# Weight blocks read in halves through attention's buffers, their size check read again beside the experts

## The chip, the cores and the metric

The kernel runs on one core of one Trainium2 chip. The metric is the device time of one execution in microseconds (us). The engines are TensorE (PE; its weight loads are PEld), VectorE (DVE), ScalarE (ACT), GpSimd (POOL) and SyncE (SP), which issues most DMAs. GpSimd has a DMA queue of its own.

## The reference

Three layers follow each other.

1. A recurrent attention for 4 batches, 8 heads, 768 steps and head size 48. A complex decay `a` is cut to a magnitude of at most 0.999; the state is `S = a * S + k v^T`, and the output is `y = q S` (its real part).
2. An MLP on the 3072 tokens of 384 numbers: `h = x @ w_in` (384 x 2048), `g = elu(h)`, `x = g @ w_out` (2048 x 384). Its two weights come as 64-bit floats.
3. A mixture of 8 experts: gates from `x @ w_gate` and a noise term, the two best experts of each token, and for each expert `relu(x @ w1[e]) @ w2[e]` (384 x 1024 and 1024 x 384), weighted and summed.

## The kernel before, in words

**Units.** Attention and MLP are cut into 12 units (6 chunks of 128 steps x 2 pairs of batches; `i` is the batch in a pair). For each unit there are pieces of work: `p` prepares the decay (a 3-buffer ring of tiles with the tag `pp`), `o` and `m` make phases and magnitudes, `a` makes the scaled keys and queries (KK, X), `b` makes scores (`sc`, tile P), the state's update (`kt`, `upd`, `upd2`; tiles KT, sx, s1), the outputs `y` and their transposed split into a high and a low part (`xt`, tiles xh and xl, from line 789). `f` is the MLP of the unit (`f_pieces`, line 817): for each of 8 steps `l1` (line 822) makes 256 rows of h and its elu in high and low parts (gh by ScalarE, gl by GpSimd, line 841), and `l2` (line 845), two steps behind, adds to the two output sums. `r` (line 954) routes the tokens of a chunk: it writes (token, gate) rows into a table in DRAM by indirect DMA (line 948).

**MLP weights.** There are 32 blocks of 128 x 384 numbers, 16 of w_in and 16 of w_out. `fetch` (line 475) issues one load of 384 KB on GpSimd's queue (line 487) into a `raw` tile. VectorE reduces the high words to their least magnitude (line 488, for the check that no weight is too small for the decoding) and decodes 64-bit floats to 32 bits in three steps (lines 471 to 473). `load_w_in` and `load_w_out` (lines 507 and 517) then split a block into a high and a low part: ScalarE copies the high part; TensorE forms `identity x raw - high` in PSUM (lines 513, 514, 525, 531), and ScalarE copies the low part out (lines 515, 532). For w_out the gate columns `w_out @ [w_gate, w_noise]` are added (three transposes, line 521, and three products, line 527). The raw tiles have the tags xh and xl, the decoded ones gh and gl, woT has the tag ge: these are buffers of the MLP. `EARLY` is 8, so that all blocks take this path and the class `x` is empty.

**Order.** `place` (line 1099) gives every piece a planned time in units from PAR, `settle` (line 1112) pushes pieces behind others by rules, and the pieces are emitted in that order. It fixes in which order tiles of one tag take its buffers. `arrange` (line 28) then orders the instructions of every engine and of SP: it simulates them with costs, takes among the ready ones that with the longest chain behind it (after the tile `gok` those of the experts' stage in order of emission), and ties each engine to that order. For a DMA it adds bytes / 190 to a common clock (line 334).

**Experts.** `e_weights` (line 1012) loads and splits an expert's weights an expert ahead; `e_slots` reads the table (line 1024), `e_rows` gathers rows (line 1035) and transposes them, `e_first` (line 1045) and `e_second` (line 1067) multiply, and rows are added to the output by indirect DMA. `check` (line 1257) stands before this stage: it reduces `guard` and `wbad`, sums over partitions by a small product and writes `flags`, which are read at the very end.

`zeros` (line 1150) fills the output and the last rows of xs by 28 DMAs from one tile with the tag yo.

The functions that the change touches, and what calls them:

Of the kernel before, what the change touches and what calls it, by code (L numbers as in the profile page):

```python
# [21 lines left out]
PAR = {'EARLY': 8, 'x': (-0.25, 0.3), 'w': (0.15, 1.0), 'p': (-0.25, 0.6), 't': (-0.2, 0.0), 'o': (-0.1, 0.2), 'm': (0.35, 0.15), 's': (0.1, 0.0), 'k': (1.0, 0.0), 'v': (0.1, 0.0), 'a': (1.2, 0.55), 'b': (1.45, 0.35), 'f': (2.1, 0.95), 'r': (2.5, 1.05), ('pr', 'p'): 1.0, ('o', 1): 0.3, ('b', 2): -0.3, ('m', 's', 7): -0.1, ('t', 2): -0.3, ('b', 's', 8): 0.1, ('p', 's', 4): 0.2, ('a', 11): -0.15, ('b', 11): -0.3, ('b', 's', 11): 0.4, ('o', 11): -0.15, ('b', 's', 6): -0.1, ('a', 1): -0.15, ('p', 1): -0.3, ('p', 's', 3): 0.1, 'z': (0.9, 0.0), 'q': (0.3, 0.0), ('b', 's', 1): 0.1, ('p', 0): 0.3, ('o', 2): -0.3, ('a', 's', 0): -0.3, ('a', 's', 4): -0.5, ('a', 's', 6): 0.1, ('a', 's', 2): 0.1, ('k', 0): 0.15, ('o', 's', 0): -0.2, ('a', 0): -0.3, ('b', 's', 4): -0.2, ('b', 's', 0): 0.2, ('b', 's', 7): -0.3, ('m', 11): -0.3, ('b', 's', 2): 0.0, ('pr', 't'): -0.5, ('f', 2): 0.15, ('b', 's', 10): 0.3, 'ring': '0000001111', 'bufs': (2, 2), ('t', 0): -0.45, ('a', 's', 3): 0.1, ('p', 's', 0): -0.1, ('f', 0): -0.15, ('pr', 'q'): 0.5, ('b', 's', 12): -0.2, ('t', 1): 0.3, ('b', 's', 5): 0.3, ('m', 's', 0): 0.2, ('pr', 'f'): -0.5, ('pr', 'x'): -1, 'fs': 0, ('q', 0): 0.45, ('a', 's', 1): 0.1, ('k', 1): 0.15, ('o', 0): -0.3, ('m', 's', 8): -0.2, ('q', 2): -0.3, ('v', 0): 0.15, ('p', 2): 0.15}  # L22
# [5 lines left out]
def arrange(tc):  # L28
# [268 lines left out]
    while done < len(heads):  # L297
# [60 lines left out]
def tile_kernel(ctx, tc, q, k, v, a_re, a_im, w_in, w_out, w_gate, w_noise, noise, w1, w2, qp, kp, vp, ap,  # L358
# [42 lines left out]
    minus = consts.tile([128, 128], F32R, name="minus")  # L401
    ts(minus, jp, 0.0, -1.0, op0=OP.is_equal, op1=OP.mult)
# [59 lines left out]
    wbad = consts.tile([128, 2, 2 * FB], F32, name="wbad")  # L462
# [823 lines left out]
    for e in range(E):  # L1286
# [3 lines left out]
        if e == 0:  # L1290
            e_slots(0, 1)
# [268 lines left out]
```

## Time and profile before

| what | us |
|---|---|
| runs | 1238.35, 1238.43, 1240.42; median 1238.43 |
| profiled execution, its own time | 1239.85 |
| its span, first to last instruction | 1238.1 |
| TensorE busy in it | 1164.2 |
| VectorE busy | 678.6 |
| ScalarE busy | 643.4 |
| GpSimd busy | 370.3 |

The span is 1.75 us shorter than the execution's own time, which includes what lies around it. Busy times are unions of an engine's records; records of TensorE and VectorE overlap at their ends. Sums of durations over a line count such overlaps twice.

### The profile page before, as it was taken

The numbers are of one execution on the slowest core, as the hardware profiler recorded it, in microseconds if no ns is written. First come the engines' busy times: TensorE is split into PE (matmuls) and PEld (weight loads), VectorE is DVE, ScalarE is ACT, GpSimd is POOL, SyncE is SP. The second block draws the span as 40 slices with busy tenths as digits, with TensorE's granted clock in tenths as the row PEclk, the third lists the DMA queues.
The fourth block names the chain that finished last, engine by engine and source line by source line (L and its number), as shares of the span: only waits on it lengthen the run. The fifth ranks groups of instructions, "written<-read, shape, count | busy, mean of one in ns | idle before, by whom it ended". The sixth has DMA issues, their size and how long they took to land.

```text
span 1238.1 us, 23439 instructions
## 1 busy us (share of the span) xinstructions
PE 1164.2 (94%) x9205; PEld 1076.3 (87%) x9205; DVE 678.6 (55%) x1454; ACT 643.4 (52%) x1299; POOL 370.3 (30%) x360
## 2 busy tenths in 40 slices
PE   4688999999999999999999999899999999999997
PEld 3466888989998999899899998889898989899996
DVE  5889887586575848658513364443434344343221
ACT  6887977767776766675544462332323233232211
POOL 2111111223215222412533633342424242424222
PEclk9788999999999999999999999899999999999999
DMA  5456423022020211201010142342424242433111
GB/s 200 148 171 199 151 80 94 16 89 68 29 74 23 80 53 59 73 23 46 15 40 14 52 135 81 117 132 87 135 89 139 84 136 83 139 99 90 37 45 34
DMA packets 64312, 107.10 MB, mean 87 GB/s; under 512 B 19967, under 2 KB 46310, under 8 KB 64192
## 3 DMA queue, kind: packets, MB, share of 16 engines
q1 hardware_dynamic: 50096, 65.65, 17.2%
q0 software_dynamic: 14096, 39.86, 10.6%
q8 instruction: 74, 1.21, 0.4%
q14 instruction: 46, 0.38, 0.1%
HBM read 86.98 MB, written 20.70 MB: 87 GB/s over the span
## 4 chain that ended last, share of the span: by engine, by line
PE 68%; issue 11%; DVE 9%; ACT 5%; POOL 4%; DMA 2%; POOLq 0%; SPq 0%; DVEq 0%; ACTq 0%
PE mpo L1077 18%; PE mph L1055 17%; PE y L855 12%; PE ph L831 11%; PE sc L759 2%; PE py L776 2%; POOL table L948 2%; PE mtp L1040 1%; POOL gl L841 1%; PE py L782 1%; PE pu L719 1%; POOL raw L487 1%; PE tp L606 1%; DMA xr<-xs,slots 1%; ACT ge L835 1%
## 5 line engine op out<-in xcount | busy, mean ns | idle before, releaser
L841 POOL TENSOR_TENSOR gl<-ge,gh 128x512 fp32r<-128x512 f32 x96 | 129.6, 1353 | 428.6 <-ACT gh L840 331.6
L1057 ACT ACTIVATE egh<-mph 128x320 fp32r<-128x320 f32 (+1 forms) x128 | 66.2, 517 | 233.2 <-PE mpo L1077 134.2
L1077 PE MATMUL mpo<-weh,egh 128*128 128x384 f32 (+1 forms) x448 | 152.4, 340 | 0.0
L1077 PE MATMUL mpo<-weh,egl 128*128 128x384 f32 (+1 forms) x448 | 152.1, 340 | 0.0
L1077 PE MATMUL mpo<-wel,egh 128*128 128x384 f32 (+1 forms) x448 | 151.8, 339 | 0.0
L855 PE MATMUL y<-woh,gh 128*128 128x400 f32 x384 | 138.8, 361 | 0.0
L855 PE MATMUL y<-woh,gl 128*128 128x400 f32 x384 | 133.0, 346 | 1.0 <-POOL gl L841 0.9
L855 PE MATMUL y<-wol,gh 128*128 128x400 f32 x384 | 131.6, 343 | 0.0
L837 DVE SCALAR_TENSOR_TENSOR ge<-ge,ph 128x512 f32<-128x512 f32 x96 | 65.4, 684 | 115.9 <-ACT ge L836 107.5
L1085 POOL DMA_INDIRECT out_dram<-ac,slots x56 | 55.7, 994 | 230.3 <-DVE ac L1082 206.6
L1058 DVE SCALAR_TENSOR_TENSOR egl<-mph,egh 128x320 fp32r<-128x320 f32 (+1 forms) x128 | 75.1, 586 | 86.3 <-ACT egh L1057 51.7
L1082 DVE SCALAR_TENSOR_TENSOR ac<-mpo,slots,ac 128x384 f32<-128x384 f32 (+1 forms) x49 | 30.2, 616 | 163.1 <-PE mpo L1077 163.1
L1008 ACT ACTIVATE weh<-raw 128x384 fp32r<-128x384 f32 x128 | 65.3, 523 | 87.5 <-PE mpo L1077 60.0
L831 PE MATMUL ph<-xh,wih 128*128 128x256 f32 x576 | 103.2, 288 | 3.0 <-DVE ge L837 3.0
L831 PE MATMUL ph<-xh,wil 128*128 128x256 f32 x576 | 100.1, 283 | 0.0
L831 PE MATMUL ph<-xl,wih 128*128 128x256 f32 x576 | 100.0, 282 | 0.0
L831 PEld LDWEIGHTS ph<-xh,wih 128*128 128x128 f32 x576 | 86.4, 189 | 6.0 <-DVE ge L837 4.3
L1009 DVE TENSOR_TENSOR wel<-raw,weh 128x384 fp32r<-128x384 f32 x128 | 73.0, 586 | 30.4 <-ACT weh L1008 23.5
L840 ACT ACTIVATE gh<-ge 128x512 fp32r<-128x512 f32 x96 | 60.0, 628 | 54.2 <-PE y L855 49.9
L835 ACT ACTIVATE ge<-ph 128x512 f32<-128x512 f32 x96 | 56.5, 593 | 60.0 <-PE ph L831 36.6
L1077 PEld LDWEIGHTS mpo<-wel,egh 128*128 128x128 f32 (+1 forms) x448 | 81.3, 182 | 2.9
L1077 PEld LDWEIGHTS mpo<-weh,egl 128*128 128x128 f32 (+1 forms) x448 | 81.2, 181 | 2.7
(199 smaller groups left out, 2703.2 us busy)
## 6 DMA issues: line engine op xcount, KB each, us to landing
raw<-in_moe_w_dram SPq DMA_DIRECT2D x128, 192.0 KB
nat_a<-in_a_rows_dram SPq DMA_DIRECT2D x24, 512.0 KB
raw<-in_moe_w_in_dram POOLq DMA_DIRECT2D x16, 384.0 KB
raw<-in_moe_w_out_dram POOLq DMA_DIRECT2D x16, 384.0 KB
q<-in_q_pairs_dram SPq DMA_DIRECT2D x24, 256.0 KB
k<-in_k_pairs_dram SPq DMA_DIRECT2D x24, 256.0 KB
vt<-in_v_rows_dram SPq DMA_DIRECT2D x24, 192.0 KB
out_dram<-zero SPq DMA_DIRECT2D x24, 192.0 KB
```

Source lines behind the costliest of these rows:

```text
L831: mm(ph[:, j, :], w[:, z, :], x[:, z, :], start=n == 0, stop=n == 3 * KD - 1)
L835: act(e, ph, AF.Relu, scale=-1.0)
L837: stt(e, e, -1.0, ph, op0=OP.add, op1=OP.max)
L840: act(gh, e, AF.Copy)
L841: nc.gpsimd.tensor_tensor(gl, e, gh.bitcast(F32), op=OP.subtract)
L855: mm(d["y"][i], g[:, j, i * L:(i + 1) * L], w, start=s == 0 and j == 0 and n == 0, stop=s == NS - 1 and j == 1 and n == 2)
L1008: act(w[0], raw, AF.Copy)
L1009: tt(w[1], raw, w[0].bitcast(F32), op=OP.subtract)
L1055: mm(ph[:, :n], w[:, z, :], x[:, z, :], start=k == 0, stop=k == 3 * KD - 1)
L1057: act(gs[0][:, f, :n], ph[:, :n], AF.Relu)
L1058: stt(gs[1][:, f, :n], ph[:, :n], 0.0, gs[0][:, f, :n].bitcast(F32), op0=OP.max, op1=OP.subtract)
L1077: mm(po[:m], x[:, f, o:o + m], w, start=k == 0, stop=k == 3 * FE - 1)
```

## The change

1. `fetch` loads a block in two halves of 192 columns on SP's queue. The raw halves take the attention's tags s15 (two of three; 4 buffers) and KT (one of three; 2 buffers), the decoded block takes pp (3 buffers), woT takes P. The reduction is gone from it, and so is `late`.
2. The low part is a subtraction on GpSimd (for the 16 gate columns on VectorE); the identity and minus products and the copies of the low part are gone.
3. The blocks are placed over 2.7 units instead of 1.0, and tied by rules only to the l1 and l2 steps that need them. The rule that put them ahead of the first `xt` is gone.
4. `upd2` is emitted right after `upd`. `zeros` takes the tag route and stands between the first and the second routing.
5. The planner's DMA rate is 300 instead of 190.
6. In the stage of experts 0 to 5, 6, 6, 6, 6, 6 and 2 blocks are loaded whole once more on SP's queue into six buffers, and VectorE reduces each to its least magnitude; the end of the check stands in expert 7.

```diff
-PAR = {'EARLY': 8, 'x': (-0.25, 0.3), 'w': (0.15, 1.0), ...
+PAR = {'w': (0.15, 2.7), ...
...
-    for new, old in (("mw", "wa"), ("mps", "psa"), ("mpo", "psf")):
+    for new, old in (("mw", "wa"), ("mps", "psa"), ("mpo", "psf"), ("mc", "wf")):
...
-                dma = max(dma, st + 600) + nbytes[z] / 190
+                dma = max(dma, st + 600) + nbytes[z] / 300
...
-    def fetch(piece, f, n, late):
-
-        tagf = "ge" if late else ("gh", "gl")[n % 2]
-        t = wf.tile([128, Dm], F32, name="wf", tag=tagf, bufs=2)
+    def fetch(piece, f, n):
+
+        t = wa.tile([128, Dm], F32, name="wf", tag="pp", bufs=3)
...
-        for z, (a, b) in enumerate(((0, 256), (256, Dm)) if late else ((0, Dm),)):
...
-                raw = wf.tile([128, Dm, 2], I32, name="raw", tag=("xh", "xl")[n % 2], bufs=2)
-            nc.gpsimd.dma_start(*piece(f, a, b, raw))
-            nc.vector.tensor_reduce(wbad[:, z, n:n + 1], raw[:, :, 1].bitcast(F32), axis=AX.X, op=OP.min,
-                                    apply_absolute_value=True)
-            decode(raw, t[:, a:b])
+        for z in range(2):
+            tag = ("s15", "s15", "KT")[(2 * n + z) % 3]
+            raw = wa.tile([128, Dm // 2, 2], I32, name="raw", tag=tag, bufs=2 if tag == "KT" else 4)
+            o = z * (Dm // 2)
+            nc.sync.dma_start(*piece(f, o, o + Dm // 2, raw))
+            decode(raw, t[:, o:o + Dm // 2])
         return t
...
+    def load_w_in(f):
         WI[f] = [wts.tile([128, KD, 128], F32R, name=f"wi{x}", tag="wi") for x in "hl"]
         hi, lo = (w.rearrange("p c f -> p (c f)") for w in WI[f])
+        raw = fetch(w_in_piece, f, f)
         act(hi, raw, AF.Copy)
-        p = psf.tile([128, Dm], F32, name="wlo", tag="ph" if late else "y2", bufs=2)
-        mm(p, ident, raw, start=True, stop=False)
-        mm(p, minus, hi, start=False, stop=True)
-        act(lo, p, AF.Copy)
+        nc.gpsimd.tensor_tensor(lo, raw, hi.bitcast(F32), op=OP.subtract)
...
+        act(wT.rearrange("p c f -> p (c f)"), p[:, :Dm], AF.Copy)
         for c in range(KD):
-            mm(p[:, Dm:], wT[:, c, :], wg[:, c, :], start=False, stop=False, skip_group_check=True)
+            mm(p[:, Dm:], wT[:, c, :], wg[:, c, :], start=c == 0, stop=c == KD - 1, skip_group_check=True)
         act(hi[:, :Dm], raw, AF.Copy)
+        nc.gpsimd.tensor_tensor(lo[:, :Dm], raw, hi[:, :Dm].bitcast(F32), op=OP.subtract)
         act(hi[:, Dm:], p[:, Dm:], AF.Copy)
-        mm(p, minus, hi, start=False, stop=True, skip_group_check=True)
-        act(lo, p, AF.Copy)
+        tt(lo[:, Dm:], p[:, Dm:], hi[:, Dm:].bitcast(F32), op=OP.subtract)
...
-        zero = wf.tile([128, Dm], F32, name="zero", tag="yo", bufs=1)
+        zero = wf.tile([128, Dm], F32, name="zero", tag="route", bufs=1)
...
-    rules += [(("w", 0), at("b", 0, "xt")), (at("a", 0, "qq", 1), ("x", 0)), (("x", 0), ("k", 1)), (("x", 0), ("q", 1)),
-              (("z", 0), at("f", 0, "fin"))]
-    for sx in range(EARLY, NS):
+    rules += [(("r", 0), ("z", 0)), (("z", 0), ("r", 1))]
+    for sx in range(NS):
...
+    def weights_seen(e):
+
+        if not wide or e > E - 3:
+            return
+        n = -(-2 * FB // (E - 2))
+        for f in range(e * n, min((e + 1) * n, 2 * FB)):
+            raw = M["c"].tile([128, Dm, 2], I32, name="seen", tag="seen", bufs=6)
+            nc.sync.dma_start(*(w_in_piece(f, 0, Dm, raw) if f < FB else w_out_piece(f - FB, 0, Dm, raw)))
+            SEEN.append((f, raw))
+
+    def weights_least():
+        while SEEN:
+            f, raw = SEEN.pop(0)
+            nc.vector.tensor_reduce(M["bad"][:, f:f + 1], raw[:, :, 1].bitcast(F32), axis=AX.X, op=OP.min,
+                                    apply_absolute_value=True)
...
     for e in range(E):
         if e + 1 < E:
             e_weights(e + 1)
+        weights_seen(e)
         e_first(e, 0)
+        weights_least()
+        if e == E - 1:
+            check_end()
```

## Rows read from the trace of the kernel before

**Rows 1.** The page, part 1: busy time, share of the span, instructions.

```profile
PE 1164.2 (94%) x9205; PEld 1076.3 (87%) x9205; DVE 678.6 (55%) x1454; ACT 643.4 (52%) x1299; POOL 370.3 (30%) x360
```

**Rows 2.** Stretches: length; PE, PEld, DVE, ACT, POOL busy; PE clock, DMA share, GB/s.

```profile
0.00:75.00 75.00, 46.02 (x267) 34.18 (x269) 54.70 (x130) 56.48 (x117) 14.39 (x32) 0.86 0.55 175
75.00:123.00 48.00, 39.31 (x286) 29.75 (x283) 46.52 (x106) 38.60 (x90) 6.99 (x13) 0.86 0.59 183
...
740.00:800.00 60.00, 54.08 (x295) 48.81 (x294) 27.69 (x90) 20.45 (x49) 21.99 (x22) 0.94 0.37 106
800.00:1238.10 438.10, 428.90 (x2385) 393.31 (x2383) 159.70 (x298) 114.86 (x245) 144.62 (x143) 0.99 0.32 95
```

**Rows 3.** Timeline of VectorE, 60 to 130 us: start, length, instruction.

```profile
76.92 1.28 DVE L763 TENSOR_TENSOR P<-sc,causal 128x512 f32<-128x512 f32 x2
...
105.57 0.36 DVE L471 TENSOR_SCALAR wf<-raw 128x384 uint32<-128x384 uint32 x1
105.84 0.55 DVE L488 TENSOR_REDUCE wbad<-raw 128x1 f32<-128x384 f32 x1
106.30 0.55 DVE L472 SCALAR_TENSOR_TENSOR wf<-raw,wf 128x384 uint32<-128x384 uint32 x1
...
127.86 0.34 DVE L741 TENSOR_TENSOR St<-sx,s 128x192 f32<-128x192 f32 x1
```

**Rows 4.** Lines 798 and 831: least, median, most ns; first and last start, us.

```profile
L798 DVE TENSOR_TENSOR xl<-tp,xh x24: 543/557/558, 112.6 to 659.2; 128x384 fp32r<-128x384 f32 x24
...
L831 PE MATMUL ph<-xh,wih x576: 274/282/388, 126.9 to 732.1; 128*128 128x256 f32 x192
```

**Rows 5.** Groups by line and form, 0 to 300 us: busy us, mean ns, idle before.

```profile
L488 DVE TENSOR_REDUCE wbad<-raw 128x1 f32<-128x384 f32 x32 | 17.4, 544 | 0.0
...
L513 PE MATMUL wlo<-wf,ident 128*128 128x384 f32 x32 | 17.2, 625 | 21.4 <-DVE wf L473 20.2 <-ACT wol L532 0.8 <-ACT wil L515 0.2
L525 PE MATMUL wlo<-wf,ident 128*128 128x384 f32 x32 | 16.6, 607 | 0.0
...
L514 PE MATMUL wlo<-wih,minus 128*128 128x384 f32 x16 | 11.2, 698 | 2.7 <-ACT wih L511 2.7
...
L531 PE MATMUL wlo<-woh,minus 128*128 128x400 f32 x16 | 7.2, 447 | 0.3 <-ACT woh L530 0.3
```

**Rows 6.** The chain that ended last, in order of time: start, length, work.

```profile
713.72 2.14 PE ph L831 x18
...
724.51 2.17 PE y L855 x12
```

**Rows 7.** Stretches of line 513 alone: PE and PEld busy, then as in rows 2.

```profile
75.00:123.00 48.00, 7.59 (x16) 2.65 (x16) 0.86 0.59 183
```

**Rows 8.** Groups by line and form, 123 to 200 us; last, a timeline row.

```profile
L673 DVE TENSOR_TENSOR KK<-KK,X 128x1024 f32<-128x1024 f32 x5 | 7.2, 1436 | 5.9 <-ACT X L582 5.9
...
L681 DVE TENSOR_TENSOR X<-X,E 128x1024 f32<-128x1024 f32 x4 | 5.9, 1487 | 0.0
...
L740 DVE TENSOR_TENSOR sx<-sx,al 128x384 f32<-128x384 f32 x5 | 3.8, 768 | 0.0
...
L565 DVE TENSOR_TENSOR nat_a<-nat_a,pc 128x384 f32<-128x384 f32 x4 | 3.3, 824 | 0.5 <-ACT pc L563 0.5
L739 DVE TENSOR_TENSOR s<-sx,al 128x384 f32<-128x384 f32 x5 | 2.8, 552 | 0.0
...
L841 POOL TENSOR_TENSOR gl<-ge,gh 128x512 fp32r<-128x512 f32 x9 | 13.1, 1455 | 76.2 <-ACT gh L840 76.2
...
159.55 2.29 DVE L673 TENSOR_TENSOR KK<-KK,X 128x1024 f32<-128x1024 f32 x1
```

**Rows 9.** Waits: who for whom; total us, times, longest us.

```profile
POOL raw L487 <- DVE wf L471: 46.0, 15, 7.2
```

**Rows 10.** The tile zero: its 24 DMAs to the output, ns, first and last start.

```profile
L1154 SPq DMA_DIRECT2D out_dram<-zero x24: 421/440/932, 73.9 to 143.2; - x24
```

**Rows 11.** The chain that ended last, in expert 0: start, length, work.

```profile
767.38 0.21 DMA slots<-table
```

More of the change, by code (lines that the diff above doesn't have):

```diff
@@ L461, in tile_kernel @@
     wide = w_in.dtype != F32
-    wbad = consts.tile([128, 2, 2 * FB], F32, name="wbad")
-    nc.vector.memset(wbad, 1.0)
     SMALL = 2.0 ** -15 * 1.125
@@ L473, in decode @@
         stt(ti, low, 29, ti, op0=OP.logical_shift_right, op1=OP.bitwise_or)
[L475 to L478 removed]
+    def fetch(piece, f, n):
+        t = wa.tile([128, Dm], F32, name="wf", tag="pp", bufs=3)
         if not wide:
[L480 removed]
+            nc.sync.dma_start(*piece(f, 0, Dm, t))
             return t
[L482 to L490 removed]
+        for z in range(2):
[4 more added lines that the diff above has]
+            decode(raw, t[:, o:o + Dm // 2])
         return t
@@ L517, in load_w_out @@
-    def load_w_out(f, late):
-        raw = fetch(w_out_piece, f, FB + f, late)
-        tp = psf.tile([128, KD, 128], F32, name="wtp", tag="ph", bufs=2)
-        for c in range(KD):
-            nc.tensor.transpose(tp[:, c, :], raw[:, c * 128:(c + 1) * 128], ident)
-        wT = wf.tile([128, KD, 128], F32, name="woT", tag="ge", bufs=2)
-        act(wT, tp, AF.Copy)
-        p = psf.tile([128, WC], F32, name="wlo", tag="ph" if late else "y2", bufs=2)
-        mm(p[:, :Dm], ident, raw, start=True, stop=False, skip_group_check=True)
+        nc.gpsimd.tensor_tensor(lo, raw, hi.bitcast(F32), op=OP.subtract)
@@ L526, in load_w_out @@
+    def load_w_out(f):
+        hi, lo = WO[f] = [wts.tile([128, WC], F32R, name=f"wo{x}", tag="wo") for x in "hl"]
+        raw = fetch(w_out_piece, f, FB + f)
+        p = psf.tile([128, WC], F32, name="wtp", tag="ph", bufs=2)
+        for c in range(KD):
+            nc.tensor.transpose(p[:, c * 128:(c + 1) * 128], raw[:, c * 128:(c + 1) * 128], ident)
+        wT = wa.tile([128, KD, 128], F32, name="woT", tag="P", bufs=2)
+        act(wT.rearrange("p c f -> p (c f)"), p[:, :Dm], AF.Copy)
         for c in range(KD):
-            mm(p[:, Dm:], wT[:, c, :], wg[:, c, :], start=False, stop=False, skip_group_check=True)
@@ L1168, in tile_kernel @@
     NS = FB // 2
-    EARLY = PAR.get("EARLY", NS)
-    wp = {False: [], True: []}
+    wp = []
     for sx in range(NS):
-        late = sx >= EARLY
         for g in (load_w_in, load_w_out):
             for f in (2 * sx, 2 * sx + 1):
-                wp[late].append((1.0, lambda g=g, f=f, late=late: g(f, late)))
-    place("w", 0, wp[False])
-    place("x", 0, wp[True])
+                wp.append((1.0, lambda g=g, f=f: g(f)))
+    place("w", 0, wp)
     fk = [x for s in range(NS + LAG) for x in ([(1, s - LAG)] if s >= LAG else []) + ([(0, s)] if s < NS else [])]
@@ L1279, in check @@
         nc.vector.tensor_copy(flags[:, 2:], counts)
-        top = wf.tile([128, 1], F32, name="top", tag="r_g4", bufs=1)
+        top = M["c"].tile([128, 1], F32, name="top", bufs=1)
         nc.vector.tensor_reduce(top, counts, axis=AX.X, op=OP.max)
@@ L1284, in tile_kernel @@
     sf.close()
+    M["c"] = sm.enter_context(tc.tile_pool(name="mc", bufs=1, reuse_waits="tile"))
+    M["bad"] = M["c"].tile([128, 2 * FB], F32, name="bad", bufs=1)
+    nc.vector.memset(M["bad"], 1.0)
     M["o"] = sm.enter_context(tc.tile_pool(name="mpo", bufs=3, space=PSUM, reuse_waits="tile"))
```

34 lines of the change are left out of this document (13 added, 21 removed).

## The prediction

> **What bounds the kernel now.** I read the page first. TensorE is busy 1164.2 of 1238.1 us [rows 1], so the run is its work plus 73.9 us of idle time, and the question is where that idle time lies. The table by stretches answers it [rows 2]: in the first 75 us TensorE is busy 46.02 us, so 29.0 us idle; from 75 to 123 us it is busy 39.31 of 48, so 8.7 us idle; the first expert (740 to 800) has 5.9 us idle, and from 800 on 428.90 of 438.10 is busy, the rest being the tail. From 75 to 123 us VectorE is busy 46.52 of 48: there VectorE sets the pace, and TensorE waits for it.
>
> What fills VectorE there is seen in the timeline [rows 3]: attention's operations with, between them, the four of one weight block, and there are 32 blocks. What TensorE lacks meanwhile is the first MLP unit, f(0). Attention of unit 0 hands its last P tile on at 76.92 to 78.2 us [rows 3], but the first xl tile of that unit starts at 112.6 us and f(0)'s first matmul at 126.9 us [rows 4]. The code says why: the weights' raw tiles have the tags xh and xl, their decoded tiles gh and gl, so x(0) has no buffer until the last blocks are through. This start-up is where the change must win; the experts' stage can only lose.
>
> **The change, part by part.**
>
> *TensorE.* The identity and minus products go, 32 records each of L513 and L525 and 16 each of L514 and L531: 17.2 + 16.6 + 11.2 + 7.2 = 52.2 us of busy time [rows 5]. The transposes and gate products stay. But nearly all of the 52.2 us lies before 123 us, where VectorE sets the pace, so removing it alone leaves idle time in its place. It counts only as far as other work fills the hole. That other work is f(0): eight pairs of l1 (18 matmuls, 2.14 us) and l2 (12 matmuls, 2.17 us) [rows 6], 8 x 4.31 = 34.5 us. Raw tiles now lie in attention's buffers, so x(0) can be made when attention is done: after 78 us, some 4 us for y, its copy, the transposes and the split, about 82 us. From 82 to 123 us there are 41 us. TensorE was busy 39.31 x 41/48 = 33.6 us of them; less half of the 52.2 us (16 of L513's 32 records lie from 75 to 123 us [rows 7], so 26 x 41/48 = 22 us) leaves 12 us. So 29 us are free. Blocks keep coming until about 120 us, and l2 trails l1 by two steps, so I take 26 us of f(0) done ahead of 123 us. That, plus about 1.5 us of removed products that lay after 123 us, is the gain: **27.5 us**, with 0 and 36 as ends.
>
> *VectorE.* A block costs, from start to start, 0.27 (shift) + 0.46 (reduction) + twice 0.47 (the other two steps have records of the same length as the reduction's) = 1.67 us [rows 3]. In halves: the 192-column operation on record is 0.34 us, less the same 0.08 us of overlap 0.26; the shift of a half is between 0.135 and 0.27, taken as 0.17. Two halves: 2 x (0.17 + 0.26 + 0.26) = 1.38 us. With 16 small subtractions at about 0.1 us: 32 x 1.67 = 53.4 becomes 45.8, so **8 us** less (bounds: 0, if shifts don't shrink, and 10).
>
> *GpSimd.* Low parts come by 32 subtractions of 384 columns. The nearest row is gl: 9 of 128x512 at 1.455 us in the busy stretch from 123 to 200 us [rows 8]; 384/512 of it is 1.09 us, 35 us in all. GpSimd has room; it has 7 to 14 us of work per stretch there [rows 2]. What it costs others is VectorE's time. In the same stretch one L673 takes 2.29 us, beside a gl; the five sum to 7.2, so the other four take 1.23, and it lost 1.06 us. L681 (1487 against 1230, x4), L740 (768 against L739's 552, x5) and L565 (824 against 552, x4) each hold one such loss. Four losses of about 1.07 us for nine gl: 0.48 us each; times 384/512 and 32 is **12 us**, with ends 0 and 35. The Trainium skill (SBUF — State Buffer, "Who interferes with whom") says more than the mean does: an operation of VectorE with two SBUF inputs and one of GpSimd that reads SBUF exclude each other for a whole instruction, and whoever comes second blocks. By that each of the 32 could cost VectorE its full length; that is a rival below.
>
> *ScalarE* loses 32 low copies, which helps a little on chains; I count nothing.
>
> *Queues.* 32 loads of GpSimd's queue become 64 on SP's, where attention's a, q, k and v loads also stand, in order. GpSimd's queue waited 46.0 us in all, up to 7.2 us at once, for one decode step to release raw tiles [rows 9]. A like wait now holds up attention's loads, and the rings s15, KT and pp tie blocks to attention's own tiles. Bounds: 0, if loads are early enough, and twice 7.2, one such wait in each of two units; I take **4 us**. The zero writes (28 issues, 0.44 us, from 73.9 us on [rows 10]) move behind the first routing: 12.3 us of SP's time beside later loads; 0 to 6, taken as **1 us**. They also leave the start-up, uncounted. The planner's new DMA rate reorders everything; that is left to the range.
>
> *Experts' stage.* 32 more loads (12.6 MB) and 32 reductions of 0.54 us [rows 5], 17.4 us on VectorE. After 800 us VectorE is busy 159.70 of 438.10 and DMA engines 0.32 of the time [rows 2], so both are covered by TensorE's work; if that cover were gone they would cost 17.4 us. The tender spot is expert 0: slots are read at 767.38 us [rows 11], and gathers and transposes wait for them. SP may put six seen loads (2.36 MB) first; at the 183 GB/s of [rows 2] that is up to 13 us. But those tiles need only old MLP buffers, so on the chip they can start earlier. I take **2 us**, 0 to 10. The end of the check moves to expert 7, under TensorE's work: nothing; without that cover, about the time of two of those reductions, 1 us.
>
> Sum: 27.5 gained, VectorE 8 - 12 = 4 lost, 4, 1 and 2 lost: 16.5 us. The profiled execution took 1239.85 us (span and 1.75 us around it), so 1223.4; the median of the runs is 1.4 us below that execution: **1222 us**.
>
> **Rivals.**
>
> *Slower: GpSimd's subtractions block VectorE.* Place: 20 to 120 us, where VectorE has no spare time. Price: all 35 us in place of 12, so 23 us more, and 16.5 gained becomes 6.5 lost: 1245 us. It decides from 28.5 us on, 0.89 us per subtraction. For: every loss in [rows 8] is nearly a whole instruction. Against: four in nine, and GpSimd may come second and wait itself. 0.14. The page of the Trainium skill named above, taken at full length, gives this case.
>
> *SP's queue.* Waits for ring buffers hold up attention's loads by 10 to 25 us instead of 4: 1228 to 1243, about 1236. For: the waits of [rows 9]. Against: three blocks are still in flight. 0.18.
>
> *Expert 0's slots come late* behind the seen loads, 13 us instead of 2: 1233. 0.06.
>
> *It streams only on paper:* rings tie x(0) to late blocks, f(0) starts near 120 us as before, and the removed products turn into idle time: 27.5 falls to about 8 by a lighter VectorE, and 1241 is left. 0.07.
>
> **How the numbers follow.** A measurement of this kernel can tell about 0.2% (2.5 us) from no change: below 1236 is faster, above 1241 slower. Forecast 0.55, all faster, 1203 to 1231 (at the good end 36 for 27.5 and next to nothing for the lock, 8.5 + 11 us better; at the other 18.5 for 27.5). Late slots 0.06 faster. SP's queue 0.18 splits into 0.07 faster, 0.05 same, 0.06 slower. The lock's 0.14 is slower. On paper only: 0.02 same, 0.05 slower. Together faster 0.68, same 0.07, slower 0.25. The range runs from the gain's good end, 1203, to just past the lock's rival, 1246.
>
> **What would show it.** Right: f(0)'s first matmul near 82 us; TensorE's idle time before 123 us at some 66 us instead of 37.7 while its busy time falls by 52; gl and the low-part subtractions beside stretched VectorE operations, some 12 us in all; stages from 800 us on as long as before. Wrong: f(0) after 110 us; a, q or k loads standing on SP's queue behind raw loads with ScalarE or VectorE waiting for them; VectorE's decode steps with means far above 0.35 us; expert 0 longer by more than 5 us.

## The result, and the profile after

The changed kernel takes **1249.56 us** (median; 1248.95 to 1251.56), the kernel before 1238.45. The ratio is 1.0083, with a 95% interval of 1.0065 to 1.0102: slower by 0.8%, where the forecast was 1222 us. The profiled execution took 1249.14 us with a span of 1247.4 us, 9.3 more than before.

The page first, part 1 (against [rows 1]):

```profile
PE 1144.8 (92%) x9109; PEld 1067.6 (86%) x9109; DVE 715.8 (57%) x1565; ACT 634.0 (51%) x1267; POOL 396.6 (32%) x360
```

TensorE is busy 19.4 us less, yet the span is longer. Where the 9.3 us went is seen from the end backwards. The last matmuls of the kernel before, and then of the changed kernel, by line (least, median, most ns; first and last start):

```profile
L1077 PE MATMUL mpo<-weh,egl x448: 332/340/522, 760.5 to 1228.6; 128*128 128x384 f32 x128, 128*64 128x384 f32 x22
```
```profile
L1064 PE MATMUL mpo<-weh,egl x448: 331/340/342, 767.0 to 1230.4; 128*128 128x384 f32 x128, 128*64 128x384 f32 x22
```

The last product starts only 1.8 us later. The other 7.5 us come after it, where no engine computes. GpSimd's sequencer there runs one instruction on its DMA counters (0.72 us before, 2.27 after) and then a drain of its queue. These are its drains, before and after, three in each kernel; the longest (the last of the three figures in ns) is the one meant, and a short one still follows it:

```profile
L1555 POOLq DRAIN  x3: 46/103/2192, 1234.7 to 1237.8; - x3
```
```profile
L1564 POOLq DRAIN  x3: 46/103/8562, 1237.9 to 1247.1; - x3
```
```profile
L1504 POOLq INC_SWDGE_SEM  x1: 2275/2275/2275, 1235.6 to 1235.6; - x1
```

The two together, called **the closing** from here on, took 0.72 + 2.19 = 2.91 us before and 2.27 + 8.56 = 10.84 after: +7.9 us.

Then the stretches of the changed kernel (columns as in [rows 2]), with their sum up to 375 us, and the experts' stage:

```profile
0.00:75.00 75.00, 32.32 (x152) 27.66 (x153) 58.72 (x167) 51.29 (x102) 25.23 (x27) 0.89 0.52 165
75.00:123.00 48.00, 35.72 (x312) 31.37 (x312) 40.38 (x106) 26.14 (x61) 18.73 (x13) 0.78 0.37 112
123.00:175.00 52.00, 46.09 (x438) 41.85 (x437) 43.46 (x93) 39.87 (x80) 16.59 (x12) 0.97 0.25 77
175.00:300.00 125.00, 120.17 (x1399) 113.70 (x1398) 103.62 (x215) 100.58 (x196) 31.00 (x24) 1.00 0.37 114
300.00:375.00 75.00, 72.42 (x838) 68.63 (x838) 57.95 (x108) 56.18 (x115) 13.45 (x10) 1.00 0.20 64
sum 375.00, PE 306.72 PEld 283.21 DVE 304.14 ACT 274.06 POOL 105.00; mean PE 61.34 PEld 56.64 DVE 60.83 ACT 54.81 POOL 21.00
```
```profile
740.00:800.00 60.00, 55.37 (x311) 49.90 (x310) 36.62 (x103) 20.48 (x48) 22.84 (x23) 1.00 0.72 246
800.00:1247.40 447.40, 430.50 (x2397) 394.30 (x2395) 170.94 (x327) 118.56 (x252) 145.48 (x145) 0.98 0.34 103
```

The middle stretches and the sum of the kernel before:

```profile
123.00:175.00 52.00, 48.26 (x610) 44.37 (x609) 47.88 (x89) 44.29 (x93) 7.75 (x5) 1.00 0.43 143
175.00:300.00 125.00, 119.31 (x1234) 113.38 (x1233) 83.29 (x181) 90.18 (x172) 32.55 (x26) 1.00 0.17 52
300.00:375.00 75.00, 74.87 (x842) 71.91 (x842) 53.34 (x106) 56.08 (x115) 13.14 (x10) 1.00 0.21 67
sum 375.00, PE 327.78 PEld 293.59 DVE 285.73 ACT 285.63 POOL 74.81; mean PE 65.56 PEld 58.72 DVE 57.15 ACT 57.13 POOL 14.96
```

Up to 375 us TensorE is busy 21.1 us less, and so idle 21.1 us more: 13.7 us of that before 75 us, 3.6 from 75 to 123. VectorE is busy 18.4 us more, though its 32 reductions (17.4 us [rows 5]) have left this part. And f(0), the goal of the change, did start early (against [rows 4]):

```profile
L786 DVE TENSOR_TENSOR xl<-tp,xh x24: 541/557/559, 82.3 to 662.6; 128x384 fp32r<-128x384 f32 x24
...
L818 PE MATMUL ph<-xh,wih x576: 274/282/416, 97.0 to 737.3; 128*128 128x256 f32 x192
```

Its first matmul is 29.9 us ahead. The lead does not last. The copies yo end each unit; from 320 to 400 us, before and then after, the last of them belongs to f(3):

```profile
L867 ACT ACTIVATE yo<-y x4: 472/483/488, 323.4 to 378.4; 128x384 f32<-128x384 f32 x4
```
```profile
L854 ACT ACTIVATE yo<-y x3: 485/487/490, 319.7 to 378.7; 128x384 f32<-128x384 f32 x3
```

At f(3) both kernels are level, 378.4 and 378.7 us. In between, unit 1 comes late. The copies xh from 120 to 200 us, two for each unit, before and after; the first one listed is the first of unit 1:

```profile
L797 ACT ACTIVATE xh<-tp x4: 470/486/486, 134.2 to 183.5; 128x384 fp32r<-128x384 f32 x4
```
```profile
L785 ACT ACTIVATE xh<-tp x3: 470/482/491, 148.1 to 193.3; 128x384 fp32r<-128x384 f32 x3
```

And the second of unit 1, before and after (start, length):

```profile
140.66 0.47 ACT L797 ACTIVATE xh<-tp 128x384 fp32r<-128x384 f32 x1
```
```profile
171.82 0.47 ACT L785 ACTIVATE xh<-tp 128x384 fp32r<-128x384 f32 x1
```

The attention of unit 1 ends 14 us (first copy) and 31 us (second copy) later than before. By the starts of each unit's last yo the lead melts over three units: 29.6 us at f(0), 14.5 at f(1), 6.5 at f(2), none at f(3). It doesn't stop there: f(11) ends 6.5 us later than before, for which no cause was found, and the experts' stage, shown further below, makes up for most of that. So there are two questions: what sets the closing, and what made unit 1 late.

### The profile page after: what moved, and what is told of

It reads as the page before. It is cut to its first block, busy times and chain, and to the rows that moved or that the text cites. A ratio compares the mean times of both kernels' runs of the same rounds, so it can differ in the third digit from the quotient of the medians.

```text
span 1247.4 us, 23498 instructions
## 1 busy us (share of the span) xinstructions
PE 1144.8 (92%) x9109; PEld 1067.6 (86%) x9109; DVE 715.8 (57%) x1565; ACT 634.0 (51%) x1267; POOL 396.6 (32%) x360
## 4 chain that ended last, share of the span: by engine, by line
PE 70%; DVE 12%; ACT 9%; DMA 4%; issue 3%; POOL 1%; POOLq 0%; DVEq 0%; SPq 0%; ACTq 0%
PE mpo L1064 18%; PE mph L1042 17%; PE y L842 12%; PE ph L818 12%; PE sc L747 2%; PE py L764 2%; DVE E L622 1%; PE mtp L1027 1%; PE tp L593 1%; PE py L770 1%; DMA nat_a<-in_a_rows_dram 1%; DVE wf L469 1%; DVE wf L467 1%; DVE wf L468 1%; DVE ge L824 1%
## 5 line engine op out<-in xcount | busy, mean ns | idle before, releaser
L842 PE MATMUL y<-woh,gh 128*128 128x400 f32 x384 | 140.0, 365 | 0.0
L842 PE MATMUL y<-woh,gl 128*128 128x400 f32 x384 | 135.3, 352 | 4.2 <-POOL gl L828 4.1
L842 PE MATMUL y<-wol,gh 128*128 128x400 f32 x384 | 133.4, 347 | 0.0
L818 PE MATMUL ph<-xh,wih 128*128 128x256 f32 x576 | 105.0, 291 | 2.7 <-DVE ge L824 2.0
L818 PE MATMUL ph<-xl,wih 128*128 128x256 f32 x576 | 100.9, 284 | 0.2
L818 PE MATMUL ph<-xh,wil 128*128 128x256 f32 x576 | 100.6, 284 | 0.0
L818 PEld LDWEIGHTS ph<-xh,wih 128*128 128x128 f32 x576 | 87.4, 192 | 5.5 <-DVE ge L824 3.5
L818 PEld LDWEIGHTS ph<-xl,wih 128*128 128x128 f32 x576 | 83.1, 192 | 0.6 <-DVE xl L786 0.6
```

What stands on the lines that cost most here:

```text
L818: mm(ph[:, j, :], w[:, z, :], x[:, z, :], start=n == 0, stop=n == 3 * KD - 1)
L842: mm(d["y"][i], g[:, j, i * L:(i + 1) * L], w, start=s == 0 and j == 0 and n == 0, stop=s == NS - 1 and j == 1 and n == 2)
```

## The experiments

All ratios are against the kernel before, measured beside each version on the same chip; the changed kernel's is 1.0083 [1.0065, 1.0102].

Two things limit what one comparison can tell. First, `arrange` orders the instructions of every version anew. Apart from the spare DMAs, the order on every engine is the changed kernel's in e5, that of e2 in e6, and that of e3 in e13 and e18; in e11 a few operations of VectorE, ScalarE and SP stand elsewhere, and in e1, e2, e4, e7 and e14 TensorE's order differs too. Second, equal orders don't give equal times: by its ratio and its closing e5 is some 3.8 us better than the changed kernel, and e13 some 7 us worse than e3. Differences of a few us between two versions are therefore hints, and only larger or repeated ones are more.

### One part at a time: queue, low parts, second read

**e1**, the halves on GpSimd's queue; **e2**, the kernel before with its whole blocks on SP's:

```
e1  -            nc.sync.dma_start(*piece(f, o, o + Dm // 2, raw))
e1  +            nc.gpsimd.dma_start(*piece(f, o, o + Dm // 2, raw))
e2  -            nc.gpsimd.dma_start(*piece(f, a, b, raw))
e2  +            nc.sync.dma_start(*piece(f, a, b, raw))
```

> The changed kernel, with the 64 loads of half blocks on GpSimd's queue instead of SP's. The changed kernel's last matmul ended at 1230.7 us of its span and 16.6 us followed; before it was 1228.9 and 9.1, and the difference lies in the closing drain of GpSimd (8.56 against 2.19 us). Theory A, the closing part grows because GpSimd's queue issues 32 loads fewer: about 9 us follow the last matmul here, time near 1242. Rival B, it grows for another reason (subtractions on GpSimd, the second read, the late end of the check): 16 us follow. Theory C, SP's queue holds up attention's loads: the last matmul ends 4 us or more earlier here. Rival D, the lock between VectorE and GpSimd ate the gain: the last matmul ends within 3 us of 1230.7 or later.

> The kernel before, with its 32 whole-block loads on SP's queue instead of GpSimd's, nothing else. Theory A: some 16 us follow the last matmul instead of 9.1, so 7 us slower by that alone. Rival B: 9 us follow. Theory C: the last matmul ends 4 us or more later than 1228.9. Rival D: within 3 us of it.

e1: 1257.36 us, 1.0149 [1.0126, 1.0172], slower than the changed kernel. Its last product starts at 1242.9 us, 12.5 later; the closing was 6.3. e2: 1243.22 us, 1.0038 [1.0028, 1.0049], slower than before, although its last product starts 6.7 us earlier:

```profile
L1077 PE MATMUL mpo<-weh,egl x448: 331/340/522, 754.4 to 1221.9; 128*128 128x384 f32 x128, 128*64 128x384 f32 x22
```

Its drain shows why: the 8562 ns of the changed kernel, to the nanosecond, and the two issue the same number of DMAs on GpSimd's queue. So the closing hides what the move gains. The 6.7 us are those of one execution, the fastest of e2's nine; by the ratios, less what lies behind the last product, the gain is 2.7 us in e2, and 4.4 and 2.3 in e6 and e14 below. Both e1 and e2 speak for SP's queue. But each of the two edits also puts other lines at more than 1000 of TensorE's some 9100 places, and queue and order were not separated.

```profile
L1555 POOLq DRAIN  x3: 46/103/8562, 1229.4 to 1238.5; - x3
```

**e3**, the low parts subtracted on VectorE (L504, and L517 likewise); **e4**, no second read:

```
e3  -        nc.gpsimd.tensor_tensor(lo, raw, hi.bitcast(F32), op=OP.subtract)
e3  +        tt(lo, raw, hi.bitcast(F32), op=OP.subtract)
e4  -        if not wide or e > E - 3:
e4  +        if True:
```

> The changed kernel, with the 32 low-part subtractions on VectorE instead of GpSimd. Theory D (the lock): the decode steps fall from 331, 382 and 421 ns to about 260, 350 and 350 ns, VectorE is relieved of some 29 us of stretching and takes on 32 x 0.47 = 15 us, and the last matmul ends 3 to 10 us earlier than 1230.7. Rival, the stretching costs nothing because VectorE is not what TensorE waits for: the last matmul ends later, by up to 10 us. If subtractions on GpSimd make the closing part long, 9 us follow the last matmul; by theory A 16 us do.

> The changed kernel without the second read of the weights and its reductions; the check of the weights' sizes is left out, its end still stands in expert 7. If the second read costs time in the experts' stage, expert 2 starts earlier by the 0 to 10 us that I had allowed; I expect less than 2 us. If it makes the closing part long, 9 us follow the last matmul; by theory A 16 us do.

e3: 1242.81 us, 1.0028 [1.0012, 1.0044], 0.55% better than the changed kernel by the two ratios. VectorE does 32 more operations itself and the kernel gains; its last product starts 5.0 us earlier, within the 3 to 10 expected. e4 leaves out the check of the sizes: 1251.63 us, 1.0104 [1.0083, 1.0125]. The second read costs nothing that shows.

### The closing

Page part 6 gives the DMAs of GpSimd's queue: in the changed kernel 56 + 56 + 49 + 48 + 2 = 211, before 32 more, in e1 64 more. I added K tiny ones that nobody reads:

```
+    spare = consts.tile([128, K], F32, name="spare")
+    for j in range(K):
+        nc.gpsimd.dma_start(spare[:, j:j + 1], w2[0, j * 128 % 1024:j * 128 % 1024 + 128, j:j + 1])
```

**e5**: the changed kernel, K = 6. **e6**: e2, K = 6. **e7**: the kernel before, K = 60.

> The changed kernel with six tiny GpSimd-queue DMAs added at the start (each 128 x 4 bytes, read by nobody), so that GpSimd's queue issues 217 DMAs in all instead of 211. Nothing else changes. Theory T (the time from the last store to the program's end, 14.8 us in the changed kernel and 7.4 in the one before, is set by how many DMAs GpSimd's queue has issued, counted modulo about 108: 211, 243 and 275 issued gave 10.8, 2.9 and 6.3 us of closing): 217 is 2 x 108 + 1, closing near 0, the span 9 to 11 us shorter than the changed kernel's 1247.4, so some 1239 to 1241 us in time. Rival U (more DMAs on that queue make the closing shorter or longer by a smooth amount, or it depends on what the last DMAs were): 1249 to 1250, as the changed kernel.

> The kernel before with its weight loads (whole blocks) moved from GpSimd's to SP's queue, and six tiny DMAs added on GpSimd's queue, 217 there in all. With the loads moved alone the last product ended 6.7 us earlier than in the kernel before, while the closing got 7.4 us longer (1243.2 us in time). Theory T: closing near 0, the gain of the queue shows, 1229 to 1233 us, faster than both kernels. Rival U: 1242 to 1244.

> The kernel before with 60 tiny DMAs added on GpSimd's queue at the start (303 in all, 303 modulo 108 is 87). Theory T: closing 9.1 us instead of 2.9, so 6 us slower plus the up to 3 us that issuing 60 DMAs at the start may cost: 1244 to 1248. Rival U1 (fewer DMAs, longer closing, smoothly): as before or shorter, 1236 to 1239.

e5: 1245.37 us, 1.0058 [1.0035, 1.0081]. e6: 1243.22, 1.0032 [1.0013, 1.0050]. e7: 1247.88, 1.0081 [1.0055, 1.0106]. Six more made the closing longer in both (11.5 us), so the restart that I expected at 216 isn't there; sixty more made it 9.3 as expected. **e11**, the changed kernel with K = 24:

> The changed kernel with 24 tiny DMAs added at the start on GpSimd's queue, 235 in all. The closing (GpSimd's last two instructions of the queue) took 10.8 us with 211 issued, 11.6 with 217, 2.9 with 243, 6.3 with 275 and 9.3 with 303: 0.105 to 0.12 us for each one issued, with a fall of some 11.4 us somewhere between 217 and 243. Theory T (a count that starts again): 2.1 us of closing, the end 8.7 us nearer to the last product than in the changed kernel, 1238 to 1243 us with the few us that issuing 24 DMAs may cost. If the fall lies between 235 and 243: closing 13.4, 1250 to 1254. Rival U (it falls with something else that only the kernel before's own loads bring): closing 12 to 13, 1250 to 1254.

e11: **1238.15 us, 1.0001 [0.9978, 1.0025]**, level with the kernel before; its last product starts 3.1 us earlier and its drain is short:

```profile
L1567 POOLq DRAIN  x3: 46/103/1457, 1232.9 to 1235.2; - x3
```

**e13** is e3 with K = 10, **e14** is e2 with K = 16:

> The changed kernel with the low parts subtracted on VectorE (as in e3: 7 us faster than the changed kernel) and 10 spare DMAs on GpSimd's queue, 221 issued in all. Closing by the line through the counts 235, 243, 275 and 303 (2.0, 2.9, 6.3, 9.3 us): 0.4 us, if the fall lies between 217 and 221. Theory T with that: 1231 to 1234 us, faster than both kernels. If the fall lies above 221: closing 12 us, 1243 to 1246.

> The kernel before with its loads on SP's queue (e2: last product 6.7 us earlier, closing 10.8) and 16 spare DMAs, 227 issued. Closing 1.1 us, if the fall lies below 227: 1231 to 1235 us. With e6 (217 issued, closing 11.6, 1243.2 us) as the other point: if the fall lies above 227, 1243 to 1245. If the queue's gain was chance: 1237 to 1239.

e14: 1236.06 us, 0.9972 [0.9961, 0.9984], faster than both kernels. Its drain took 0.72 us, that of e13 9.46:

```profile
L1558 POOLq DRAIN  x3: 46/103/722, 1230.6 to 1231.9; - x3
```
```profile
L1567 POOLq DRAIN  x3: 46/103/9460, 1233.5 to 1243.5; - x3
```

All drains by the number of DMAs issued on GpSimd's queue:

| issued | 211 | 217 | 221 | 227 | 235 | 243 | 275 | 303 |
|---|---|---|---|---|---|---|---|---|
| drain, ns | 8562 | 9133 | 9460 | 722 | 1457 | 2192 | 4887 | 7337 |
| closing, us | 10.8 | 11.5 | 12.0 | 1.1 | 2.0 | 2.9 | 6.3 | 9.3 |

The drain climbs by 82 to 95 ns for each DMA and falls once, between 221 and 227. Kernels of one number agree to the nanosecond whatever else they do (211: the changed kernel, e2, e3, e4). Theory T holds but for the place of the fall. With 227 the last store also starts some 1.5 us later, so that 8.3 to 8.6 us lie between the start of the last product and the end, about as with 235 (8.0 and 8.2); before it was 9.5, in the changed kernel 17.0. e13 took 1250.64 us (1245.7 to 1256.47), 1.0098 [1.0078, 1.0118]: the closing explains 1.1 us against e3, and some 7 more stay open. Its trace doesn't show them: the profiled execution, 1245.70 us, is the fastest of its six, and its last product starts at 1225.6 us, e3's at 1225.4. **e18** repeats it with K = 16 and a short closing:

> The changed kernel with the low parts subtracted on VectorE and 16 spare DMAs (227 issued, closing 1.1 us). If e3's gain is real: 1230 to 1234 us. If e13 told the truth and e3 was chance: 1237 to 1241 us, as the changed kernel with its closing short.

e18: **1234.22 us, 0.9951 [0.9934, 0.9968]**, the fastest version that computes everything, faster than both kernels. e3's gain shows again, against e11 with a short closing by 0.5%; e13, with the same order of instructions, is the odd one out, and why is open. (The profiled execution of e18 took 1241.57 us, the slowest of its eight, so nothing is read from its trace but the drain, 722 ns.)

### VectorE and the rings

**e9** leaves out the low parts (the low products read zeros; the weights count with their high part alone). **e10** leaves out the third decode step (the last three bits of the mantissa are zero). **e15** leaves out both. In e9 the line shown goes with L517 and L519, and w_out is treated like w_in.

```
e9   +    wz = [wts.tile([128, KD, 128], F32R, name="wiz", tag="wi"), wts.tile([128, WC], F32R, name="woz", tag="wo")]
e9   +        WI[f] = [wts.tile([128, KD, 128], F32R, name="wih", tag="wi"), wz[0]]
e9   -        nc.gpsimd.tensor_tensor(lo, raw, hi.bitcast(F32), op=OP.subtract)
e10  -        stt(ti, low, 29, ti, op0=OP.logical_shift_right, op1=OP.bitwise_or)
```

> The changed kernel without the low parts: the 32 subtractions on GpSimd (32 x 1.24 to 1.5 us) and the 16 small ones on VectorE are left out, and the low products read a tile of zeros, so the weights count with their high part alone; the products themselves all stay. Theory L (GpSimd's subtractions stretch VectorE's operations beside them: VectorE was occupied 18.4 us longer up to 375 us although 14.8 us of reductions had left it, so some 29 to 33 us in all, and this ate what f(0)'s early start won): f(3) ends 12 to 30 us earlier than at 375.6 us, the time falls to 1220 to 1238 us. Rival R (the attention of unit 1 is late since the raw loads take turns with it in the rings kt and s15, and not through VectorE's work): f(3) ends within 5 us of 375.6, 1243 to 1250 us.

> The changed kernel with two of the three decode instructions for each half: the third one, which puts the low word's three highest bits into the float, is left out (64 x some 0.42 us = 27 us of VectorE), so the last three bits of the weights' mantissa are zero. The lock, the loads and the rings stay. Theory V (VectorE's work in the first 375 us sets f(1) to f(3)): f(3) ends 12 to 27 us earlier, 1222 to 1238 us. Theory L strictly (only the lock with GpSimd counts): some of that, as fewer operations are stretched, 5 to 15 us. Rival R: within 5 us of the changed kernel.

> The changed kernel with both e9's and e10's cuts: no low parts (they read zeros; no subtraction on GpSimd, none of the 16 small ones on VectorE) and two of three decode instructions. Alone they ended f(3) at 370.9 and 366.6 us against 375.6, and the time fell by 7.3 and 8.3 us. Theory V (VectorE's work bounds the first units, the cuts add): f(3) near 360 us, 1232 to 1236 us. Rival R (behind VectorE stands another bound: rings, loads or TensorE at the lower clock; the cuts don't add): f(3) at 365 to 369, 1239 to 1243 us.

e9: 1242.23 us, 1.0022 [0.9997, 1.0048]. e10: 1241.23, 1.0018 [0.9996, 1.0040]. e15: 1234.25, 0.9956 [0.9944, 0.9969]. By the ratios that is 0.61%, 0.65% and 1.27% better than the changed kernel: the cuts add, as theory V said, though each is smaller than forecast, and e9 and e10 alone are little more than the scatter named above. At f(3) the three are 4.7, 6.9 and 11.0 us earlier, the first and the last within what the rivals R had allowed. The decode shift of the changed kernel, and of e9:

```profile
L467 DVE TENSOR_SCALAR wf<-raw x64: 225/253/1332, 8.9 to 154.9; 128x192 uint32<-128x192 uint32 x64
```
```profile
L470 DVE TENSOR_SCALAR wf<-raw x64: 241/250/265, 9.0 to 151.9; 128x192 uint32<-128x192 uint32 x64
```

The medians are the same, but eight of the 64 shifts of the changed kernel took 451 to 1332 ns, most of them beside a low-part subtraction (up to 1084 ns; the longest is beside a gl). In e9 none took over 265. Up to 375 us, e9 and then e15:

```profile
sum 375.00, PE 314.89 PEld 293.59 DVE 290.94 ACT 276.50 POOL 61.07; mean PE 62.98 PEld 58.72 DVE 58.19 ACT 55.30 POOL 12.21
```
```profile
sum 375.00, PE 316.29 PEld 294.42 DVE 280.41 ACT 280.96 POOL 64.20; mean PE 63.26 PEld 58.88 DVE 56.08 ACT 56.19 POOL 12.84
```

VectorE lost 13.2 us in e9 and 23.7 in e15, and the time fell by about 7.6 and 15.7 us (the ratios' differences times 1238): some 0.6 us for each us that VectorE is freed of. In e10 it is 0.4 (19.5 us and 8.0).

**e8** lets the schedule stream the weights as early as before. **e16** keeps the raw halves out of the ring KT: all 64 go through the four buffers of s15 instead of s15 and KT's two.

```
e8   -PAR = {'w': (0.15, 2.7),
e8   +PAR = {'w': (0.15, 1.0),
...
e16  -            tag = ("s15", "s15", "KT")[(2 * n + z) % 3]
e16  +            tag = "s15"
```

> The changed kernel with the weight stream's length in the schedule set back from 2.7 to 1.0 units, the value of the kernel before: all weights are to be there early, and the attention's pieces of unit 1 are put behind more of them. Theory (the weights' stream is held by the rings it shares with the attention, and VectorE's locked decodes make unit 1's attention late): f(0) starts a little earlier than 97 us or at the same time, unit 1's attention (first xh tile at 148 us) gets later, 1250 to 1262 us. Rival (the stream was only spread too wide, the loads come as early as asked): f(0) starts by 85 us and the time falls to 1235 to 1246.

> The changed kernel with all 64 raw halves in the ring s15 (4 buffers) and none in KT (2 buffers); in the changed kernel SyncE's queue waited 19 us between 60 and 160 us for products that read KT before a raw half could be loaded there. Theory R (the shared KT ring holds the stream and the attention of unit 1): those waits go, the last decode comes before 150 us instead of 156, f(3) 4 to 12 us earlier, 1237 to 1246 us. Rival V (the rings give way to each other, VectorE sets the pace): f(3) within 4 us, 1246 to 1251 us. Against: s15 has then 64 instead of 43 takers, so its own waits can grow and the stream be later, 1250 to 1258.

e8: 1261.46 us, 1.0180 [1.0144, 1.0216], as its theory said; but the last decode step starts at 106.4 us (156.5 in the changed kernel) and f(0) at 132 instead of 97, which neither guess had. e16: 1261.85 us, 1.0182 [1.0165, 1.0199]; both its guesses about a gain failed. SP's queue, from 40 to 160 us, in the changed kernel and in e16 (who waits for whom; total us, times, longest):

```profile
SPq L481 <- DVE wf L469: 29.2, 13, 6.7
SPq L481 <- PE pu L706: 19.0, 3, 10.2
```
```profile
SPq L481 <- DVE wf L469: 42.2, 13, 10.6
SPq L445 <- PE pu L706: 20.5, 3, 9.7
```

In the changed kernel a raw load (L481) waited for products that read KT. In e16 that wait left L481, but a load of v (L445) waited for those products, and the raw loads waited 13 us more for decode steps to give s15 back. So the rings bind the stream too: with two buffers fewer, all of them shared with the attention's s15, the time is 12 us longer. More buffers, or buffers of the stream's own, were not tried, and what the shared rings cost the changed kernel stays unpriced.

### What the removed products were worth

**e17** puts the low parts back on TensorE, as before the change, with K = 16; all else is the changed kernel (for w_out the same four lines; its 16 gate columns stay with VectorE).

```
-        nc.gpsimd.tensor_tensor(lo, raw, hi.bitcast(F32), op=OP.subtract)
+        p = psf.tile([128, Dm], F32, name="wlo", tag="ph", bufs=2)
+        mm(p, ident, raw, start=True, stop=False)
+        mm(p, minus, hi, start=False, stop=True)
+        act(lo, p, AF.Copy)
```

> The changed kernel with the low parts back on TensorE (64 products through the identity and its negative, and a ScalarE copy for each block, as in the kernel before) and 16 spare DMAs, 227 issued in all (closing 1.1 us); GpSimd subtracts nothing. Beside it the changed kernel with its closing short took 1238.2 us (24 spare DMAs). Theory I (in the first 75 us TensorE idles 43 us anyway, so those products cost little there, and the lock that GpSimd's subtractions put on VectorE cost 6 us): 1230 to 1236 us, at or below that. Rival P (the products were worth on TensorE what they took, some 23 us of the 39): 1245 to 1260 us.

e17: 1239.22 us, 0.9987 [0.9968, 1.0006]; e11, the changed kernel with a short closing, has 1.0001 [0.9978, 1.0025]. They can't be told apart, and the time lies between what theory I (to 1236) and rival P (from 1245) had said. Yet TensorE is busy 17.8 us longer than in the changed kernel:

```profile
PE 1162.6 (94%) x9205; PEld 1075.3 (87%) x9205; DVE 698.5 (56%) x1566; ACT 645.0 (52%) x1299; POOL 361.2 (29%) x344
```

So 17.8 us of TensorE's work and GpSimd's subtractions are worth the same here, to within measurement; with the subtractions at some 7 us (e9), the products cost about that too, an estimate, and well under half of the 17.8. In e17 f(3) ends at 368.5 us, ten us before the changed kernel's, and f(4) at 435.5, level with it: the end of a single unit does not measure a lead.

**e12** is e2 without its reductions in the start-up, with the second read in the experts' stage (weights_seen, weights_least and check_end as in the change) and K = 24:

```
-            nc.gpsimd.dma_start(*piece(f, a, b, raw))
-            nc.vector.tensor_reduce(wbad[:, z, n:n + 1], raw[:, :, 1].bitcast(F32), axis=AX.X, op=OP.min,
-                                    apply_absolute_value=True)
+            nc.sync.dma_start(*piece(f, a, b, raw))
...
+        weights_seen(e)
```

> The kernel before with three parts of the change or of the experiments: its loads on SP's queue (whole blocks), its 32 reductions taken out of the start-up and the second read put into the experts' stage as in the changed kernel, and 24 spare DMAs on GpSimd's queue (235 in all). The low parts stay products of TensorE, the buffers stay. Queue: 6.7 us gained; VectorE freed of 14.8 us in the start-up, worth 0 (if TensorE sets it) to 12 us (if VectorE does); second read 0; closing 2.1 us instead of 2.9. So 1220 to 1233 us, faster than both kernels; if the fall of the closing lies above 235, some 11 us more.

e12: 1238.15 us, 0.9999 [0.9984, 1.0013], 5 us above the upper end of what was expected, with the closing at the 2.0 us expected. In the old design, whose TensorE does the low parts, taking the reductions off VectorE and adding the read gained nothing; e14, without these two parts, is even 0.3% faster, though VectorE is busy 285.0 us up to 375 us there and 273.1 in e12. So the 0.6 us for each us of VectorE belong to the changed kernel alone.

## Why the prediction was wrong

**The closing: no term at all.** The sum changed nothing behind the last product: the end of the span and the 1.75 us around it were taken over from the kernel before. But moving 32 loads off GpSimd's queue took its count from 243 to 211, and that alone costs 7.9 of the 11.1 us by which the medians differ. e11 shows it: with 24 more DMAs, read by nobody, the kernel is level with the one before. Of the 11.4 us between the medians 8.8 are the closing; its trace has the last product 3.1 us earlier, and that lies in the experts' stage, which begins 1.0 us later and is 4.1 shorter than in the changed kernel. Nothing in the trace of before could have given this size; its 2.2 us drain at the end could have raised the question.

**The gain, 27.5 us: the step that failed.** It said that f(0)'s 26 us run ahead of 123 us would come off the end. The way there was right: the first xl is there at 82.3 us (predicted about 82), and f(0) starts 29.9 us earlier. But it missed the second xh of that unit, at 96.4 us, for which the first matmul waits, and less of f(0) was done ahead of 123 us; here are l1 (L818) and then l2 (L842) in that stretch, busy time and matmuls first:

```profile
75.00:123.00 48.00, 9.72 (x74) 9.14 (x75) 0.78 0.37 112
```
```profile
75.00:123.00 48.00, 5.77 (x15) 4.07 (x15) 0.78 0.37 112
```

That is 74 of 144 and 15 of 96 matmuls, 9.72 + 5.77 = 15.5 us instead of 26, and only 11.5 at the prediction's prices of 2.14 us for 18 and 2.17 for 12. Above all it missed what comes after: f(1) needs unit 1's attention, which is 14 to 31 us later than before, and the lead was gone by f(3).

The removed products were also over-counted. TensorE's busy time fell by 19.4 us over the run, not by 52.2. Records overlap: counted once, and only where no other matmul's record lies, the removed ones make 34.9 us, 33.9 of them before 123 us; the other matmuls, the same 9109 in both kernels, are busy 15.5 us longer. Idle time before 123 us is 55.0 us, and 37.7 + 33.9 - 15.5 = 56.1 accounts for it. The mark of 66 does not follow from the prediction's own terms (37.7 + 50.7 - 26 = 62.4) and counts the overlaps in full. From 75 to 123 us the granted clock was 0.78 (before 0.86 [rows 2]), so part of f(0) ran at the lower of the two levels, 1.2 GHz. What the clock cost was not tested.

**The lock, 12 us on VectorE: about right for the new subtractions, and a part missing.** e9 takes 13.2 us off VectorE up to 375 us; 1.7 are the small subtractions that went too, so 11.5. Counted in the changed kernel's trace (VectorE's records that begin while one runs and are over 0.15 us longer than the median of their form), the 32 subtractions cost 15.7 us, in 23 records. In time it was some 7 by e9. What no term had: GpSimd's gl, which both kernels have, now also meets the blocks and more of the attention. By the same count it cost VectorE 10.4 us up to 375 us before and 18.3 after. The rival that put the lock at its whole length is refuted: the 32 subtractions took 24.1 + 19.8 = 43.9 us here, not 35, and took 11.5 to 15.7 us of that from VectorE:

```profile
L504 POOL TENSOR_TENSOR wil<-wf,wih 128x384 fp32r<-128x384 f32 x16 | 24.1, 1505 | 53.4 <-ACT wih L503 43.1 <-ACT woh L518 10.3
L517 POOL TENSOR_TENSOR wol<-wf,woh 128x384 fp32r<-128x384 f32 x16 | 19.8, 1242 | 39.5 <-ACT woh L516 38.8 <-ACT woh L518 0.7
```

The Trainium skill (SBUF — State Buffer, "Who interferes with whom") says that the second comer of the two blocks for the whole instruction. The trace agrees for single ones. Here the last step of a decode, 0.35 us by its median, starts 0.19 us after a subtraction and takes 1.03 us:

```profile
32.05 1.00 POOL L504 TENSOR_TENSOR wil<-wf,wih 128x384 fp32r<-128x384 f32 x1 [0.63 <-ACT wih L503]
32.24 1.03 DVE L469 SCALAR_TENSOR_TENSOR wf<-raw,wf 128x192 uint32<-128x192 uint32 x1
```

It doesn't follow that each of the 32 meets one.

**VectorE's 8 us saved: too much.** Halves cost what was worked out: by the starts in the timeline 0.17 + 0.27 + 0.27 = 0.71 us (predicted 0.69). Counted from each start to the start of VectorE's next instruction, at most to its own end, over all blocks, decode and reduction took 54.5 us before and the halves 49.8 in e9 (58.1 in the changed kernel): 4.7 less. With 1.7 for the small subtractions, 3.0 us were saved.

**SP's queue, 4 us lost: the runs point the other way.** In the kernel before, the move gains 2.3 to 4.4 us up to the last product by the ratios (6.7 in e2's trace), and in the changed kernel the way back costs 12.5 (e1). The waits of [rows 9] do come to SP's queue (29.2 and 19.0 us above), but on GpSimd's queue the loads stand behind the subtractions, which wait for ScalarE's copies; in e1, up to 160 us:

```profile
POOL raw L481 <- DVE wf L469: 24.8, 8, 9.1
POOL wil L504 <- ACT wih L503: 15.5, 10, 3.0
POOL wol L517 <- ACT woh L516: 13.2, 6, 5.7
```

That this is why e1 loses, and not its new order, is argued, not shown apart. The Trainium skill (DMA: Bandwidth & Descriptors, "Issuing engine by pattern") gives simple loads to SyncE's queue as the faster; the times of e1, e2, e6 and e14 agree, with the order as the open rival.

**The experts' stage, 2 us: not contradicted.** The first products of expert 0, before and after:

```profile
L1055 PE MATMUL mph<-ex0h,weh x192: 390/397/501, 741.7 to 1186.7; 128*128 128x512 f32 x192
```
```profile
L1042 PE MATMUL mph<-ex0h,weh x192: 391/397/508, 746.9 to 1188.5; 128*128 128x512 f32 x192
```

From there to the last product it is 1228.6 - 741.7 = 486.9 us before and 1230.4 - 746.9 = 483.5 after, and e4 gains nothing without the second read (487.6). Over all versions, whose products in this stage are the same, it took 479.4 to 488.2 us, so 2 us can't be told here, nor is the 3.4 a gain of the change. The experts start 5.2 us later than before, which the 1.8 us at the last product hide.

**The rivals.** The measured 1249.6 lies nearest to "GpSimd's subtractions block VectorE" (1245), by accident of the closing. "It streams only on paper" is false in its mark, since f(0) started at 97.0 us, and right in its core: the removed products mostly turned into idle time. "SP's queue" and "expert 0's slots" did not come true: for the first see above, and from expert 0's first product to the first mpo (760.5 and 767.0 us, above) it was 18.8 us before and 20.1 after, 1.3 more and not 11 more. The moved zeros were not tested alone.

## What to carry to other kernels

Work taken off the busiest engine is a gain only if the next piece for it is ready too: follow a unit that starts early to the units behind it and to the engine that feeds them (here VectorE, some 0.4 to 0.7 us of time for each us in the changed kernel, nothing in e12), before its whole head start is counted. Look behind the last computing instruction when DMAs change queues, and compare versions with that part taken out, since 8 us of closing can hide a better version. Repeat a version whose order of instructions is the same before a difference of a few us is believed. Where a queue and a low part can be moved apart, as in e14 and e18, they may be worth more than the whole change.

## What the hardware showed that was not expected

The drain of GpSimd's queue at the program's end depends on how many DMAs that queue issued: 722 ns at 227 issued and some 90 ns more for each further one up to 303 (7337 ns), but 8562 ns at 211 and 9460 at 221. The closing was 12.0 us with 221 and 1.1 with 227, so six tiny transfers can make 11 us. Why it falls between 221 and 227, and whether by the number of DMAs or by something that goes with it, was not settled.
